# A gated mix of a 2-D Fourier filter and a Mish layer: the first four x tiles bypass the butterflies, the gate's exponential moves to GpSimd, and the order of all engines is written anew

## The chip, the cores and the metric

The kernel runs on one core of one Trainium2 chip. The metric is the device time of one execution in microseconds (us). Five engines work from queues of their own, each strictly in its written order: TensorE (PE in the profile; its weight loads are PEld), VectorE (DVE), ScalarE (ACT), GpSimd (POOL), and SyncE (SP), which only issues transfers.

## The reference

The input x has 2048 rows of 512. Two branches are mixed row by row by a gate:

```python
g = sigmoid((x * gate_w).sum(-1, keepdims=True))
X = rfft2(x);  a = irfft2(X * (w_r + 1j * w_i), s=(2048, 512))    # spectral branch
h = x @ w1 + b1                                                   # 512 -> 1792
act = h * tanh(log(1 + exp(h)))                                   # Mish
b = act @ w2                                                      # 1792 -> 512
out = g * a + (1 - g) * b
```

All tensors are bf16 in memory.

## The kernel before, in words

x is held as 16 tiles of 128 rows (tile t has rows t, t+16, t+32, ...). The work is cut into some 540 named tasks; each has a function that emits its instructions, the data it reads and writes, and an engine (some may go to one of two or three). What runs in which order is a text, `ORDER` (line 327): it lists the task names, and `place` (line 222) walks it once. Each task goes to the end of its engine's queue; `name:dve` picks the engine, `name::1` gives the slot of the buffer that the task opens. Three pairs of PSUM banks (pool `pr`), two single banks (`mm2`) and three SBUF buffers (`tmp`) are shared; a task that opens a slot waits for all users of its former holder. A GpSimd task waits for the GpSimd task before it, and for the last VectorE task marked `lock` that stands before it in the order. So an instruction that waits holds up everything behind it on its engine.

The tasks, in the order of the data:

- *Loads.* `x0` to `x3` bring four tiles each into rA, `w1_0` to `w1_2` the columns of w1, all on SP's queue; `cRF`, `braw`, `graw`, `cFD` (constants and biases) go over ScalarE's queue. `wr..s.` and `wi..s.` stage the filter weights in rE. `xt8` to `xt15` are transposing loads of x tiles 8 to 15, `w2_0`, `w2_1` load w2.
- *Warm-up.* `warm` is a row of 13 matmuls on zeros (line 537), fed by a memset `warm0` (line 526). `ones` and `ident` (lines 527, 529) build the identity matrix that transposes use.
- *Transposes.* `tr0` to `tr7` (line 603) turn tiles 0 to 7 on TensorE, `evx` copies them into xT.
- *Mish branch*, four chunks c of 512 rows: `mm1_c_f` (line 897, four matmuls of 512 columns for one of 14 blocks of 128 hidden features), `hc_f` (line 904 on VectorE, 908 and 909 on ScalarE: adds b1 to two blocks and empties a PSUM pair), `exp`, `ln`, `tanh` on ScalarE (lines 918, 920, 921), `mulc_half_tile` (line 933), `mm2_t_.._0` and `_1` (line 949: eight and six matmuls for one tile), `o` (line 966 or 963: times 1 - g).
- *Spectral branch, forward.* `bf` (line 618) forms on GpSimd the sum and the difference of the two halves of each row, x[0:256] +- x[256:512], the first step of the transform along the row. `p` (line 637) transforms each tile across its 128 rows, four matmuls of 128 columns for the sum and the difference, odd and even columns; `ep` empties PSUM; `d` (line 649) transforms along the row, `ed` empties it into rD. `s1w0` to `s1w3` write rD to a scratch in memory, four tiles each, and `s1r0` to `s1r3` read it back in another layout into rE, over the staged weights. So they wait for all copies that take the weights from there (`wrm...`, `wim...`, lines 684 and 685) as well. `wrn` duplicates the real part by a transfer within SBUF, `win` negates and copies the imaginary part on VectorE.
- *Filter.* `t` (line 762) is a 16-point transform, `et` empties it, `sa` and `sb` swap the halves of the partitions by DMA, `p1`, `p2`, `ad` (lines 776, 779, 782) multiply and add. An edge correction follows: `e1` (800, 801), `es0`, `es1` on ScalarE (809, 810), `xp1`, `xp2`, `ead` on VectorE (811, 812, 813), `e2` (820, 822), `e3` (826).
- *Backward.* `it` (line 837), `eit`, `id` (876), `ey`, and `ip` (line 975 for tiles 0 to 11; 957 for 12 to 15, accumulated into mm2's bank).
- *Gate.* `gate0` (tiles 0 to 11) and `gate12` (line 732), `zcl` clamps, `ez` is exp on ScalarE (line 743), `ez1` adds 1, `omg` is the reciprocal, `gcol` the product (749). `fa`, `fb`, `fin` (983, 987, 979) mix, `out` stores.

The h of chunk 2 goes into rD, which the scratch writes read: `h2_..` wait for all four `s1w`.

Of the kernel before, what the change touches and what calls it, by code (L numbers as in the profile page):

```python
# [10 lines left out]
AF = mybir.ActivationFunctionType  # L11
ALU = mybir.AluOpType
# [315 lines left out]
ones cRF x0 ident warm0 w1_0 wrp0 warm::0 braw wrp1 x1 graw w1_1 cFD w1_2 x2 x3 wr0s0 wr0s1 tr3::0 bf0_1:pool tr2::1 evx3:dve wr0s2 evx2:act tr1::0  # L328
wr1s0 tr0::1 bf2_0:pool evx1:act evx0:dve wr1s1 mm1_0_0::1 wi0s0 bf0_0:pool wi0s1 mm1_0_1 wi0s2 bf4_1:pool tr5::0 wi1s0 tr_b::1 p0::2 ev_b evx5:act p1
wi1s1 mm1_0_2::0 h0_0:dve xt8 mm1_0_3 ep0:dve bf4_0:pool mm1_0_4::1 h0_2:dve mm1_0_5 mm1_0_6::2 bf2_1:pool h0_4:dve exp0_0 p4::0 p5 mm1_0_7 bf8_1:pool  # L330
ep4:dve mm1_0_8::1 h0_6:dve p6::0 p7 mm1_0_9 bf12_0:pool ep6:dve exp0_4 mm1_0_10::2 h0_8:dve mm1_0_11 bf8_0:pool d6::0 d7 h0_10:dve d0::1 ed6:act
tr7::1 d1 tr6::0 evx7:dve mm1_0_12::2 exp0_8 evx6:dve bf12_1:pool ed0:dve mm1_0_13 p8::0 tr4::1 h0_12:dve p10::1 evx4:act p11 p9 xt9 wip1 ep8:act
ep10:dve wip0 p14::2 wrm101:pool p15 exp0_12 p2::0 p3 ep14:dve mm1_1_8::1 xt10 ln0_0 wrm110:pool mm1_1_9 ep2:dve d14::2 d15 h1_8:dve d2::0 xt11 d3
wim001:pool ed2:dve mm1_1_2::1 mm1_1_3 w2_0 ed14:dve wim111:pool d4::0 s1w0 ln0_8 d5 h1_2:dve d10::2 d11 w2_1 gate0::0 wrm111:pool ed10:dve mm1_1_4::1
tanh0_0 zcl0 mm1_1_5 ed4:dve wrm011:pool p12::2 p13 h1_4:dve mm1_1_6::0 s1w1 mm1_1_7 wrm010:dve mm1_1_0::1 wim000:dve ldM wrm000:dve mm1_1_1 rft
ep12:act wim101:dve mul0_0_3:dve h1_6:act d8::2 d9 mul0_0_0:dve mm2_3_0_0::1 mul0_0_1:dve ez0 tanh0_8 mul0_0_2:dve mm1_1_10::0 h1_0:dve wim100:pool
mm1_1_11 ed8:dve mm1_1_12::1 exp1_0 wim110:pool mm1_1_13 h1_10:dve s1w2 d12::2 d13 ez10 omg0 mm1_2_4::0 h1_12:act gcol0 mul0_1_0:dve mul0_1_1:dve
mm2_1_0_0::0 exp1_4 mul0_1_3:dve mul0_1_2:dve mm2_1_0_1 wrm100:dve exp1_8 ed12:dve wrn1 wim011:pool mm1_2_12::1 o1_0:dve s1w3 mm1_2_2::2 exp1_12
wrm001:dve mm1_2_3 win1:dve ln1_0 wrn0 mm2_2_0_0::0 wim010:dve win0:dve s1r0 mm1_2_5 s1r1 mm1_2_13 s1r2 wic1:dve wiz1:dve wic0:pool h2_2:dve s1r3
mm2_2_0_1 wiz0:pool wrc1:pool wrz1:pool edge h2_12:dve ln1_8 ldG mm1_2_6::2 wrc0:pool wrz0:pool mm1_2_7 o2_0:dve mm1_2_10::1 h2_4:dve tanh1_0 mm1_2_11  # L340
h2_6:dve mm1_2_8::0 h2_10:dve mm1_2_9 mm1_2_0::2 h2_8:dve mm1_2_1 t2_0::1 h2_0:dve xt12 t6_0::0 t6_1 tanh1_8 mul1_0_1:pool t2_1 mm2_0_0_0::0 et2:dve
xt13 t0_0::2 t0_1 mul1_0_0:dve t3_0::1 et6:act t3_1 mul1_1_1:dve mm2_0_0_1 sa2::0 mul1_0_3:dve sb2 et3:act sa6::1 t5_0::0 mul1_1_0:dve t5_1 sb6
o0_0:act t4_0::1 mul1_1_2:dve t4_1 et5:act sa3::2 mul1_1_3:dve mm2_3_0_1 sb3 et4:dve mul1_0_2:pool xt14 et0:act t7_0::0 t7_1 mm2_4_0_0::0 o3_0:dve
et7:act xt15 p2_2:dve exp2_0 mm2_4_0_1 p1_2:dve ad_2:dve t1_0::1 t1_1 p1_3:dve o4_0:act mm2_5_0_0::1 sa0::0 et1:act p2_3:dve sb0 p1_6:dve inv exp2_4
mm1_3_0::2 p2_6:dve mm1_3_2::0 ad_6:dve ad_3:dve mm1_3_12::1 sa1::1 exp2_8 p2_0:dve sb1 mm1_3_3 p1_0:dve sa4::2 mm2_5_0_1 sb4 ad_0:dve exp2_12
h3_2:dve sa5::0 gate12::0 ln2_0 sb5 mm1_3_13 p2_1:pool zcl12 o5_0:dve mm1_3_8::0 h3_12:dve mm2_6_0_0::0 p1_1:dve p2_4:dve mm2_6_0_1 p1_4:dve ln2_8
ad_4:dve mm1_3_4::1 p2_5:dve sa7::2 mm1_3_9 p1_5:dve sb7 ad_1:dve mm1_3_5 ez12 h3_8:dve ad_5:pool mm2_7_0_0::1 h3_4:dve tanh2_0 mm1_3_6::0 p1_7:dve
mm1_3_7 p2_7:dve mm2_7_0_1 ad_7:dve h3_6:dve e1::1 mm1_3_1 es0::1 mul2_0_0:pool es1 ez112 o7_0:act xp2 mm1_3_10::0 ezb12 xp1::0 tanh2_8 ead::2
mm1_3_11 o6_0:dve e2::1 mul2_0_3:pool h3_0:dve mm2_8_0_0::1 e3 exp3_0 h3_10:dve it5_0::2 it7_0::1 mul2_1_2:pool it7_1 it5_1 eit7:dve mm2_11_0_0::0
exp3_4 mul2_1_3:dve it3_0::0 eit5:dve it3_1 mul2_1_0:pool it6_0::1 it6_1 exp3_8 mm2_11_0_1 eit6:dve mul2_0_2:pool it2_0::2 it2_1 eit3:dve exp3_12  # L350
it1_0::1 it1_1 mm2_8_0_1 o11_0:dve ln3_0 mul2_0_1:pool it0_0::0 eit2:dve it0_1 mm2_10_0_0::0 eit0:dve it4_0::2 mul2_1_1:pool it4_1 o8_0:dve ezr1::0
# [10 lines left out]
LOADS = ["x0 w0 x1 w1 w2 x2 x3", "x0 x1 w0 w1 x2 w2 x3", "x0 w0 x1 w1 x2 w2 x3", "x0 w0 w1 x1 w2 x2 x3"]  # L362


def _build(nc, A_x, A_w_r, A_w_i, B_x, B_w1, B_b1, B_w2, gate_w, out, merge=12, xtp=8, xtl=12, loads=0, finb=11, nbf=0, u3=1, wdma=1):
# [10 lines left out]
    with es:  # L376
# [57 lines left out]
        warm = hs01[:, 1, 0:256]  # L434
# [5 lines left out]
        def bank(b, i=0):  # L440
            return ps[:, (2 * b.slot if b.pool == "pr" else 6 + b.slot) + i, :]
# [7 lines left out]
        def tb(b):  # L449
            return tmp[:, b.slot, :]  # L450
# [3 lines left out]
        def tf(b):  # L454
            return tmpf[:, b.slot, :]
# [70 lines left out]
        G.add("warm0", "pool", 0.2, lambda e: e.memset(warm, 0.0), "warm", writes=["warm"])  # L526
# [4 lines left out]
        NWARM = 13  # L531
        wb = _Buf("pr")

        def f_warm(e):
            ins = None
            for _ in range(NWARM):
                ins = e.matmul(bank(wb)[:, 0:256], warm[:, 0:128], warm, start=True, stop=True)
            return ins

        t_warm = G.add("warm", "pe", NWARM * 0.22, f_warm, "warm", reads=["warm"], writes=[wb])  # L540


        XG = [(0, 4), (4, 8), (8, 12), (12, 16)]
# [3 lines left out]
        def ld(name, *a, **kw):  # L547
            seq[0] += 1
            kw.setdefault("cls", "f_ld")
            return dma(name, *a, off=-0.01 * seq[0], **kw)  # L550

        def ld_x(i, **kw):
            a, b = XG[i]
            return ld(f"x{i}", x_sb[:, a:b, :], xv[:, a:b, :], 1.4 + 0.6 * (a == 0), writes=[("x", t) for t in range(a, b)], **kw)
# [5 lines left out]

        ld("cRF", cst[:, 0, :], d_front[:, 0, :], 0.2, writes=["cRF"], queue="act")
# [21 lines left out]
        for i, (a, b_) in enumerate([(0, 8), (8, 14)]):  # L583
            ld(f"w2_{i}", w2_sb[:, a:b_, :], w2v[:, a:b_, :], 0.39 * (b_ - a), cls="f_w2", nd=8 * (b_ - a), writes=[("w2", f) for f in range(a, b_)])
# [128 lines left out]
        dma("ldM", rF[:], d_M[:].rearrange("p f n -> p (f n)"), 5.6, "f_m", writes=["M"], deps=t_p[6:7])  # L713
        dma("rft", rft[:, :], d_inv[:, 0, :], 0.3, "f_late", writes=["rft"], deps=t_p[6:7])
        dma("ldG", rB[:], d_G[:].rearrange("p f n -> p (f n)"), 5.6, "f_late", writes=["G"], deps=t_p + t_s1w)
# [6 lines left out]
        for t0, t1 in ((0, 12), (12, 16)):  # L722
            gb = _Buf("mm2")
# [19 lines left out]
            add("ez", 0.3, lambda e, c_=c_: e.activation(ez[:, c_], zcl[:, c_], AF.Exp), ["zcl"], ["ez"], eng="act", tab="et")  # L743
# [3 lines left out]
            add("omg", 0.2, lambda e, c_=c_: e.reciprocal(omg[:, c_], gcol[:, c_]), ["gcol"], [("omg", t) for t in range(t0, t1)])  # L747
            if t0 < merge:
                add("gcol", 0.17, lambda e, c_=c_: e.tensor_tensor(out=gcol[:, c_], in0=ez[:, c_], in1=omg[:, c_], op=ALU.mult),
                    ["ez"] + [("omg", t) for t in range(t0, t1)], ["gcol"] + [("gc", t) for t in range(t0, t1)])  # L750
# [297 lines left out]
```

## Time and profile before

| what | us |
|---|---|
| median of 4 runs | 146.05 (144.88 to 146.13) |
| the profiled execution | 144.88 |
| its span (first to last instruction) | 142.9 |
| TensorE busy | 132.1 |
| VectorE busy | 119.6 |
| ScalarE busy | 112.8 |
| GpSimd busy | 63.3 |
| first transpose, first mm1 matmul | 5.41, 8.26 |
| last group of matmuls begins | 139.42 |

The profile is of one execution. A line of the timeline gives start, duration, engine, source line, operation, output and input, shape and count; in brackets stands the idle time of the engine before the line and what ended it. Durations of matmuls overlap, so the distance from one start to the next is their true cost. Two bf16 instructions of VectorE that follow each other overlap a little as well: the 1.22 us of an evacuation of 1024 columns cost 1.14 in a row.

### The profile page before, as it was taken

How to read it: one execution, taken by the hardware profiler on the slowest of the kernel's cores; microseconds unless marked ns; L12 is line 12 of the kernel's file. 1: busy time of each engine (PE TensorE's matmuls, PEld its weight loads, DVE VectorE, ACT ScalarE, POOL GpSimd, SP SyncE). 2: the span in 40 equal slices, each digit the busy share in tenths (PEclk: the TensorE clock that was granted, in tenths of full speed). 3: DMA queues.
4: the chain of work that ended last, by engine and by line, in shares of the span. 5: the costliest groups of instructions: out<-in, count | busy, mean ns of one | idle time of the engine just before them, and what ended most of it. 6: DMA issues, size and time to landing. Idle time of an engine off the chain costs nothing.

```text
span 142.9 us, 2342 instructions
## 1 busy us (share of the span) xinstructions
PE 132.1 (92%) x905; PEld 73.7 (52%) x921; DVE 119.6 (84%) x154; ACT 112.8 (79%) x77; POOL 63.3 (44%) x50
## 2 busy tenths in 40 slices
PE   4789999889969999998999999998699999999992
PEld 3435556657534544444665454443366567655561
DVE  0117999999999998897968999997999989899772
ACT  2211557899999999999899999998499999945470
POOL 4499996799607250304150040509639700003510
PEclk9999999999999999999999999999999999999999
DMA  3999999999979959999999680300000000000554
GB/s 103 324 373 391 169 162 165 92 216 324 281 182 408 253 116 224 318 339 399 339 231 105 162 206 8 73 0 0 0 0 0 5 0 0 0 5 0 220 197 173
DMA packets 22991, 23.45 MB, mean 164 GB/s; under 512 B 13828, under 2 KB 19716, under 8 KB 22404
## 3 DMA queue, kind: packets, MB, share of 16 engines
q1 hardware_dynamic: 22512, 23.07, 63.0%
q10 hardware_dynamic: 468, 0.23, 0.6%
q8 instruction: 7, 0.11, 0.3%
q14 instruction: 4, 0.03, 0.1%
HBM read 14.89 MB, written 4.19 MB: 134 GB/s over the span
## 4 chain that ended last, share of the span: by engine, by line
PE 68%; ACT 11%; DMA 8%; DVE 7%; issue 3%; SPq 2%; DVEq 0%
PE ps L949 30%; PE ps L897 19%; PE ps L876 5%; DMA rE<-scr 5%; ACT uT L920 4%; DMA rA<-in_A_x_dram 3%; PE ps L837 3%; PE ps L762 3%; ACT uT L921 3%; PE ps L603 2%; SPq L477 2%; DVE rA L697 2%; PE ps L975 2%; PE ps L637 2%; PE ps L649 1%
## 5 line engine op out<-in xcount | busy, mean ns | idle before, releaser
L897 PE MATMUL ps<-rX,w_sb 128*128 128x512 bf16 x216 | 51.7, 385 | 1.4 <-DVE rX L514 0.5
L949 PE MATMUL ps<-w_sb,hs 128*128 128x512 bf16 (+1 forms) x178 | 39.5, 362 | 0.2
L897 PEld LDWEIGHTS ps<-rX,w_sb 128*128 128x128 bf16 x224 | 21.5, 99 | 26.1 <-issue 1.5
L949 PEld LDWEIGHTS ps<-w_sb,hs 128*128 128x128 bf16 x182 | 17.5, 98 | 17.4 <-DVE hs L933 0.3
L904 DVE TENSOR_TENSOR hs<-ps,b1f 128x1024 bf16<-128x1024 f32 x19 | 23.2, 1226 | 1.1 <-PE ps L897 0.6
L920 ACT ACTIVATE uT<-uT 128x4096 bf16<-128x4096 bf16 (+1 forms) x6 | 19.1, 3190 | 0.1
L921 ACT ACTIVATE uT<-uT 128x4096 bf16<-128x4096 bf16 (+1 forms) x6 | 19.1, 3187 | 0.1
L618 POOL TENSOR_TENSOR rB<-rA 128x1024 bf16<-128x1024 bf16 (+1 forms) x10 | 17.3, 1734 | 4.0 <-DMA rA<-in_A_x_dram 3.3
L918 ACT ACTIVATE uT<-hs 128x2048 bf16<-128x2048 bf16 (+1 forms) x8 | 13.6, 1694 | 5.5 <-DVE hs L904 5.3
L933 POOL TENSOR_TENSOR rD<-rD,uT 128x1024 bf16<-128x1024 bf16 (+1 forms) x7 | 13.4, 1918 | 7.1 <-ACT uT L921 3.4
L949 PE MATMUL ps<-w_sb,rD 128*128 128x512 bf16 x53 | 12.7, 379 | 0.2
L983 ACT ACTIVATE tmp<-ps,gcol 128x512 bf16<-128x512 f32 x11 | 7.2, 686 | 6.6 <-PE ps L975 6.0
L987 POOL TENSOR_TENSOR rX<-rX,tmp 128x512 bf16<-128x512 bf16 x3 | 3.5, 1152 | 19.2 <-ACT tmp L983 15.3
L966 DVE TENSOR_SCALAR rX<-ps,omg 128x512 bf16<-128x512 f32 (+1 forms) x13 | 9.2, 705 | 1.4 <-PE ps L949 1.2
L514 DVE CAST rC<-ps 128x1024 bf16<-128x1024 f32 x8 | 9.6, 1217 | 0.8 <-PE ps L762 0.8
L514 DVE CAST rA<-ps 128x1024 bf16<-128x1024 f32 x8 | 9.5, 1217 | 0.6 <-PE ps L876 0.6
L514 DVE CAST rF<-ps 128x1024 bf16<-128x1024 f32 x8 | 9.5, 1212 | 0.2 <-PE ps L837 0.2
L904 DVE TENSOR_TENSOR rD<-ps,b1f 128x1024 bf16<-128x1024 f32 x7 | 8.3, 1218 | 1.5 <-PE ps L897 0.8
L918 ACT ACTIVATE rW<-hs 128x2048 bf16<-128x2048 bf16 (+1 forms) x4 | 6.8, 1698 | 2.2 <-DVE hs L904 2.0
L514 DVE CAST rD<-ps 128x1024 bf16<-128x1024 f32 x7 | 8.4, 1210 | 0.0
L517 ACT ACTIVATE rC<-ps 128x1024 bf16<-128x1024 f32 x8 | 8.0, 1017 | 0.4 <-PE ps L762 0.2
L933 POOL TENSOR_TENSOR hs<-hs,uT 128x1024 bf16<-128x1024 bf16 x2 | 4.3, 2127 | 8.9 <-ACT uT L921 5.4
(95 smaller groups left out, 191.2 us busy)
## 6 DMA issues: line engine op xcount, KB each, us to landing
rA<-in_A_x_dram SPq DMA_DIRECT2D x4, 512.0 KB, 9.1
scr<-rD SPq DMA_DIRECT2D x4, 512.0 KB, 5.7
rF<-c_m SPq DMA_DIRECT2D x1, 2048.0 KB, 11.5
rE<-scr SPq DMA_DIRECT2D x4, 512.0 KB, 6.3
rB<-c_g SPq DMA_DIRECT2D x1, 2048.0 KB, 11.4
tmp<-rC SPq DMA_DIRECT2D x16, 128.0 KB, 2.5
out_dram<-rX SPq DMA_DIRECT2D x7, 256.0 KB, 2.3
w_sb<-in_B_w_dram SPq DMA_DIRECT2D x2, 768.0 KB, 9.4
```

Of the source, the lines that this page charges most:

```text
L514: return e.tensor_copy(out=o(), in_=i())
L517: return e.activation(o(), i(), AF.Copy)
L618: return e.tensor_tensor(out=xu[:, a:b_, uv, :], in0=x_sb[:, a:b_, 0:256], in1=x_sb[:, a:b_, 256:512], op=ALU.add if uv == 0 else ALU.subt ...
L897: ins = e.matmul(bank(b, i), w1_sb[:, dt_, 128 * ft:128 * (ft + 1)], xT[:, c, dt_, :, :], start=(dt_ == 0), stop=(dt_ == 3))
L904: return e.tensor_tensor(out=hs[hb][:, ft:ft + 2, :], in0=pair(b).rearrange("p (f s) -> p f s", f=2), in1=b1f[:, ft:ft + 2].unsqueeze(2).t ...
L918: return e.activation(o, hsf[hb][:, 512 * a:512 * b_], fn_)
L920: return e.activation(o, o, fn_, bias=1.0)
L921: return e.activation(o, o, fn_)
L933: return e.tensor_tensor(out=v, in0=v, in1=uvs[c][:, a:b_, 128 * tl:128 * (tl + 1)], op=ALU.mult)
L949: ins = e.matmul(bank(b)[:, 0:hi - lo], hs[hb][:, ft, 128 * tl:128 * (tl + 1)], w2_sb[:, ft, lo:hi], start=(ft == 0), stop=(ft == NFT - 1))
L966: return e.tensor_scalar(out=bs[:, t, lo:hi], in0=bank(b)[:, 0:hi - lo], scalar1=omg[:, t:t + 1], scalar2=None, op0=ALU.mult)
L983: G.add(f"fa{t}", "act", act(512) + 0.09, lambda e, t=t, b=b, z=z: e.activation(tb(z)[:, 0:512], bank(b), AF.Copy, scale=gcol[:, t:t + 1]) ...
```

## The change

Five edits go together.

1. *No butterflies for tiles 0 to 3* (`nbf=4`). The tasks `bf0_0`, `bf0_1`, `bf2_0`, `bf2_1` are gone. `p0` to `p3` take x itself: each of the four results is accumulated from two matmuls, one per half of the row, the second with the negated matrix NRF for the difference. NRF is loaded into `rft` by a new transfer `cNRF`, and `rft`'s later content now waits for the scratch writes.
2. *Loads.* Tiles 0 to 3 come as two loads of two tiles: `x0` first on SP's queue, `x1` first on ScalarE's. The others are now `x2` to `x4`.
3. *Warm-up.* The zeros and their memset are gone; 14 matmuls of 256 columns run on the identity, as soon as that is built. The bias tasks no longer wait for the warm-up.
4. *Gate.* `ez` is no longer exp on ScalarE but a power, e to the z, on GpSimd (`tensor_tensor` with `pow`); the base is written by two new memsets, `ec0` and `ec12`. `gcol`, `xp2` and `ead` are marked `lock`.
5. *A new ORDER* for all engines, and with it other choices of engine.

```diff
-def _build(nc, A_x, ..., merge=12, xtp=8, xtl=12, loads=0, finb=11, nbf=0, u3=1, wdma=1):
+def _build(nc, A_x, ..., merge=12, xtp=8, xtl=12, loads=0, finb=11, nbf=4, u3=1, wdma=1):
...
-        G.add("warm0", "pool", 0.2, lambda e: e.memset(warm, 0.0), "warm", writes=["warm"])
...
-                ins = e.matmul(bank(wb)[:, 0:256], warm[:, 0:128], warm, start=True, stop=True)
+                ins = e.matmul(bank(wb)[:, 0:256], identt[:, :], identt[:, :].unsqueeze(1).to_broadcast([128, 2, 128]), start=True, stop=True)
...
-        XG = [(0, 4), (4, 8), (8, 12), (12, 16)]
+        XG = [(0, 2), (2, 4), (4, 8), (8, 12), (12, 16)]
...
+        ld_x(1, queue="act")
         ld("cRF", cst[:, 0, :], d_front[:, 0, :], 0.2, writes=["cRF"], queue="act")
         if nbf:
             ld("cNRF", rft[:, :], d_front[:, 1, :], 0.2, writes=["rft"], queue="act")
...
-        dma("rft", rft[:, :], d_inv[:, 0, :], 0.3, "f_late", writes=["rft"], deps=t_p[6:7])
+        dma("rft", rft[:, :], d_inv[:, 0, :], 0.3, "f_late", writes=["rft"], deps=t_s1w)
...
+            G.add(f"ec{t0}", "pool", 0.1, lambda e, t0=t0, t1=t1: e.memset(omg[:, t0:t1], math.e), "w", writes=[(("omg", "c"), t0)])
...
-            add("ez", 0.3, lambda e, c_=c_: e.activation(ez[:, c_], zcl[:, c_], AF.Exp), ["zcl"], ["ez"], eng="act", tab="et")
+            add("ez", 0.35, lambda e, c_=c_: e.tensor_tensor(out=ez[:, c_], in0=omg[:, c_], in1=zcl[:, c_], op=ALU.pow), ["zcl", (("omg", "c"), t0)], ["ez"], eng="pool")
...
-        G.add("xp2", "dve", 0.29, ..., reads=wcs[2:4], writes=[e2_])
-        G.add("ead", "dve", 0.29, ..., reads=[e1_, e2_], writes=[ey_])
+        G.add("xp2", "dve", 0.29, ..., reads=wcs[2:4], lock=True, writes=[e2_])
+        G.add("ead", "dve", 0.29, ..., reads=[e1_, e2_], lock=True, writes=[ey_])
```

The new order, engine by engine, where it matters below:

- TensorE begins `warm tr1 tr0 tr2 tr3 mm1_0_2 tr5 tr6 p2 p0 p1 mm1_0_3 tr7 p3 mm1_0_6 mm1_0_7 tr_b mm1_0_0 mm1_0_1 mm1_0_4 mm1_0_5 d2` (before: `warm tr3 tr2 tr1 tr0 mm1_0_0 mm1_0_1 tr5 tr_b p0 p1 mm1_0_2`). In the middle stand `p6 p7 gate0 d4 d5 p12 p13 d6 d7 mm1_1_0 d12 mm1_1_1 mm1_1_10 d13 mm1_1_11 d10 d11 mm1_2_0 mm1_2_1 p8 p9 d0 d1 mm2_1_0_0 d8 mm2_3_0_0`, later `mm2_2_0_1 mm1_2_3 mm2_0_0_0 mm1_2_6 mm1_2_7 mm1_2_4 mm1_2_5 mm1_2_12 mm1_2_13 t6_0`. Around the edge: `mm2_5_0_1 mm2_9_0_0 e1 mm2_10_0_0 mm2_9_0_1 e2 mm2_10_0_1 it2_0` (before: `mm2_7_0_1 e1 mm1_3_1 mm1_3_10 mm1_3_11 e2 mm2_8_0_0 it5_0`).
- VectorE: `h1_4 ep6 zcl0 ep12 ed6 ez10 omg0 h1_0 ed12 ed10 h1_10 mul0_0_1`; `h1_12 o3_0 ed8 o1_0 wim000 wim100 win1 win0 o2_0 h2_0 h2_2`; at the edge `h3_4 h3_6 xp1 h3_10 xp2 mul2_1_2 ead mul2_0_0 e3 o9_0 ezb12`.
- ScalarE: `exp0_12 ln0_0 ln0_8 ed4 tanh0_0 tanh0_8 ep8 ed0 exp1_0`; `tanh2_8 o5_0 exp3_0 es0 es1 exp3_4 exp3_8 exp3_12 eit2 ln3_0 eit7 ln3_8 tanh3_0`. `h1_6`, `h1_12` and `ep12` go from ScalarE to VectorE.
- GpSimd begins `wrp1 ones ident ec12 ec0 wrp0 bf4_0 bf4_1`; `ez0` stands between `wrm001` and `wrm010`, `ez12` between `mul2_1_1` and `mul2_1_0`.
- SP: `xt11 w2_1 w2_0 ldM s1w1 wrn0 s1w3 s1w0 wrn1 s1w2 s1r0 s1r1 s1r3 s1r2 ldG edge rft` (before: `xt11 w2_0 s1w0 w2_1 s1w1 ldM rft s1w2 wrn1 s1w3 wrn0 s1r0 s1r1 s1r2 s1r3 edge ldG`).

## The prediction

> **What bounds the kernel now.** I read the page's totals and slices first, then TensorE's timeline from end to end, then the other engines around each hole in it.
>
> ```profile
> PE 132.1 (92%) x905; PEld 73.7 (52%) x921; DVE 119.6 (84%) x154; ACT 112.8 (79%) x77; POOL 63.3 (44%) x50
> ...
> PEclk9999999999999999999999999999999999999999
> ```
>
> TensorE is the bound on average, with VectorE close behind. Since its work is nearly fixed, only its holes can be gained, and the timeline names them:
>
> ```profile
> 1.80 2.95 PE L537 MATMUL ps<-hs 128*128 128x256 bf16 x13 [1.80 <-POOL hs L526]
> 5.41 2.33 PE L603 MATMUL ps<-identt,rA 128*128 128x128 bf16 x16 [0.66 <-DMA rA<-in_A_x_dram]
> 8.26 3.01 PE L897 MATMUL ps<-rX,w_sb 128*128 128x512 bf16 x8 [0.52 <-DVE rX L514]
> ...
> 41.65 0.62 PE L649 MATMUL ps<-cst,rC 128*128 128x128 bf16 x8 [1.13 <-ACT rC L517]
> ...
> 66.52 1.05 PE L762 MATMUL ps<-rE,rF 128*128 128x128 bf16 x16 [0.41 <-DMA rE<-scr]
> ...
> 101.03 0.20 PE L820 MATMUL ps<-tmp,rD 128*128 128x1 bf16 x2 [1.61 <-DVE tmp L813]
> ```
>
> [...] From the first transpose at 5.41 to the last matmul at 140.25 are 134.8 us; 2.65 us of evacuation and output follow, and the execution took 144.88 against its span of 142.9, so 1.98 us lie outside it.
>
> Weight loads show a loss that the brackets don't:
>
> ```profile
> 8.66 0.15 PEld L897 LDWEIGHTS ps<-rX,w_sb 128*128 128x128 bf16 x1 [0.28 <-issue]
> 9.09 0.15 PEld L897 LDWEIGHTS ps<-rX,w_sb 128*128 128x128 bf16 x1 [0.28 <-issue]
> ```
>
> They come 0.427 us apart until 10.4; the 16 matmuls of the same size from 79.16 to 82.61 come 0.216 us apart. TensorE runs at half speed up to about 10.4 us, although the granted clock reads full. A 128-column matmul costs 0.056 us (t, 16 in 66.52 to 67.41), half speed 0.107.
>
> The hole at 101.03 is made by GpSimd:
>
> ```profile
> 96.50 6.11 POOL L933 TENSOR_TENSOR rD<-rD,uT 128x1024 bf16<-128x1024 bf16 x3 [3.37 <-ACT uT L921]
> 97.47 1.30 DVE L812 TENSOR_TENSOR tmp<-tmp,wsi 128x128 f32<-128x128 f32 x1 [0.87 <-ACT tmp L810]
> 99.08 1.90 DVE L813 TENSOR_TENSOR tmp<-tmp 128x128 bf16<-128x128 f32 x1
> 102.80 6.94 ACT L918 ACTIVATE rW<-hs 128x2048 bf16<-128x2048 bf16 x4 [2.00 <-DVE hs L904]
> ```
>
> xp2 (L812) and ead (L813) take 1.30 and 1.90 us while GpSimd multiplies; xp1, of the same shape but with one operand in PSUM, took 0.28. Each ends about where one of GpSimd's multiplications ends. So 1.0 + 1.6 us of VectorE are stall, e2 waits 1.6 us for them, and h3_0 behind them keeps ScalarE idle for 2.0 us.
>
> **Part 1, loads and warm-up.** Landing in the old kernel:
>
> ```profile
> rA<-in_A_x_dram SPq DMA_DIRECT2D x1, 512.0 KB, 4.6
> w_sb<-in_B_w_dram SPq DMA_DIRECT2D x1, 512.0 KB, 6.3
> ```
>
> x0 landed at 5.36 and w1_0, issued at 1.25, at 7.5. Now x0 and x1 carry half each on two queues. By 5.4 the engines had moved some 0.9 MB (slices of half a microsecond: 190 to 370 GB/s from 2.0 on), of which x0 took half. Two quarter-megabyte loads beside w1_0 end between 4.2 (they go first) and 5.1 (all share equally); I take 4.7. Four transposes and their copies took 8.21 - 5.41 = 2.8 us, bound by two PSUM banks and copies of 0.42 to 0.6; they end near 7.5, where w1_0 lands too. So the first mm1 starts at 7.5 rather than 8.26. The extra issues (x1 0.39, cNRF 0.36 on ScalarE's queue) push ScalarE's table load, 2.69 to 3.97 today, to about 4.7; its first copy is due at 6.5. A warm-up matmul costs 0.213 us. It now waits for the identity, which GpSimd builds after one 0.27 us memset: 1.37 + 0.27, so fourteen run from about 1.7 to 4.7. GpSimd's two new memsets come after and stand in front of an addition that waits for x2 until 9.1.
>
> [...] the 2.9 us of half-speed work that I see up to 10.4 would shrink by 1.4. By the row, 2.95 us of warm-up, 0.66 of idleness and gappy transposes did not release it until 10.4. The new transposes have the same gaps, so I take 0 and keep the 1.4 for the range.
>
> **Part 2, no butterflies for four tiles.** GpSimd loses four additions of 1.15 us, 4.6 in all; TensorE gains 16 matmuls: 16 x 0.056 = 0.9 us, up to 1.7 if all were cold. GpSimd isn't the bound; what it buys is that p0 to p3 need only x, so that they fill TensorE at 9 to 13 us.
>
> **Part 3, the new order, by checkpoints.** I walk down TensorE's new queue with 0.865 us for an mm1 task, 1.73 / 1.30 for mm2 halves, 0.45 for two p or d, and let it wait for a PSUM pair where VectorE's queue (1.14 to 1.22 us per evacuation) frees it later.
>
> At 35.35 the new queue has finished d4 and d5. Against the old at 34.94 it has done four mm1 more (3.46), six d (1.35) and two p (0.45) less: 1.66 of useful work in 0.41 longer, **1.25 us ahead**. ScalarE's chain: exp0_12 ends near 26.4 (was 28.03), ed4 waits for d5 until 35.4, tanh0_8 ends at 44.1 (was 45.5).
>
> h1_6, h1_12 and ep12 move from ScalarE (2 x 1.27 and 0.92 off) to VectorE (3 x 1.14 on), ed6 too, ed0 and ed4 the other way; the walk carries them. From 36 to 44 VectorE sets the pace: h1_0, ed12, ed10 and h1_10 free the pairs; TensorE waits 0.4 before mm1_2_0 and 0.7 before p8. That is the old hole of 1.13, not removed but equalled.
>
> ed8 ends near 53.6, so s1w2 goes out then (s1w3 did at 51.67) and lands after the old 5.9 us at 59.5; s1r2 follows and lands near 66, as the last s1r did (66.17). Two waits stand here. h2_0 waits for s1w2 until 59.5, and on VectorE behind it stand all of h2, mul1 and the filter products; mm1_2_6 needs its pair at 60.9 and gets it at 60.7. rft, now behind ldG on SP's queue, is wanted only past 112, and w2 and M come in earlier than needed (mm2_1_0_0 at 44.5, t6_0). t6_0 waits for s1r2; TensorE reaches it at 66.1. By then it has done 14 mm2 matmuls more and 8 mm1 matmuls less than the old at 66.5: +1.3, and 0.4 earlier, **1.7 ahead**.
>
> From t6_0 to e2 the work is 16 mm1 tasks (13.85), 84 mm2 matmuls (18.15), t 3.6, gate 0.45, e1 0.3: 36.35, so e2 comes at 102.4. VectorE from h2_0 to e3: 39.9 us of instructions from 59.5, against 41.8 over 45.4 in the old; it fits with the old idleness of 3.6. The locks on xp2 and ead hold back GpSimd's next instruction, ez12, until they are done (behind ez12 stand mul2_1_0 and mul2_0_3, needed at 107 and 110), and mul2_1_1 ends near 100.3, before xp2 can start (exp3_0 stands before es0, so es1 ends near 100.9). xp2 and ead at 0.3 each with mul2_1_2 between finish at 102.0. e2 waits for nothing: the 1.6 us is the gain, **3.3 ahead**.
>
> After e2 remain 90 mm2 matmuls (19.4), it 3.6, id 7.0, ip 3.5, ezr 0.2: 33.7, plus the old 0.7 of small gaps: 136.9 instead of 140.25. What is late next is ScalarE: exp3_0 starts at 98 instead of 102.8, tanh3_0 ends near 119.8 with the two evacuations eit2 and eit7 added; mm2_12_0_0 can start at 120.5 and 15.6 us of work follow it. Both chains meet within half a microsecond.
>
> **Part 4, the power.** Off ScalarE go 0.22 and 0.21 us. GpSimd's own memsets and the power itself are not in the trace. Nearest row:
>
> ```profile
> L618 POOL TENSOR_TENSOR rB<-rA 128x512 bf16<-128x512 bf16 x4 | 4.6, 1151 | 3.3 <-DMA rA<-in_A_x_dram 3.1
> ```
>
> With 2.12 for 1024 elements this gives 0.18 + 0.0019 per element: 0.2 for twelve. Lower end 0.2. [...] the first TENSOR_TENSOR took as long as its sisters. By the row ez0 (zcl0 ends at 35.8) is done near 36.2, two microseconds before VectorE wants ez10; I take 0.4. [...]
>
> **Sum.** 1.25 by the front, 0.45 in the s1r stage, 1.6 at the edge: 3.3, less 0.3 for handovers a walk doesn't see: 3.0. The profiled 144.88 would become 141.9; the median of 146.05 becomes 143.0.
>
> **Rivals.**
> *Clock released early* (0.1): a further 1.4 off, 141.6. For it: the longer, later warm-up; against it: gaps between transposes.
> *Later scratch write takes the front's gain* (0.22): the second rW copy stands directly ahead of s1w2 in SP's queue, and in the old trace one such copy took 0.54 us to issue and one 2.64. With 2.64, h2_0 and t6_0 slip by 1.2 to 2, VectorE has no slack to return it: 144.2 to 145.
> *The split does not speed x* (0.1): landing still near 5.3 and w1_0 late, front gain near 0.4: 143.9 to 145.4, to no change with a second slip.
> *The power is slow* (0.06, slower): at c us each, VectorE loses c - 2.4 at ez10 and c - 1.2 at ezb12; beyond c = 3.4 the whole gain is gone, [...] against it the first-call row.
>
> **Numbers.** My forecast of 143.0 has 0.52. Its own spread is 142 to 144; for eight in ten I reach down for the clock and up for the slip: 141.2 to 145.4. Measurement tells about 1% (1.5 us). Faster by more: forecast, clock and most of the two slips, 0.84; within: 0.10; slower: 0.06.
>
> **What would show it.** Right: first mm1 at 7.3 to 7.8; t (L762 now) at 66 with more mm2 before it; no idle time ahead of e2, xp2 and ead at 0.3; last matmul near 137. Wrong: weight loads 0.2 apart before 10 us (clock); idle time ahead of mm1_2_6 (slip); VectorE waiting for GpSimd at ez10 or ezb12 (power).

## The result, and the profile after

The changed kernel takes **142.16 us** (median of 11 runs, 141.31 to 143.54); the kernel before took 144.84 beside it (16 runs, 142.93 to 146.13). The ratio is 0.986 with a 95% interval of 0.981 to 0.991: faster, by about 1.4%. The ratios in this document leave out executions more than 1.5% above a kernel's fastest, and of the kernel before that drops many, so they show less gain than the medians do; both are given. The profiled execution took 143.38, with a span of 141.7 (before 144.88 and 142.9).

Totals on the page of the changed kernel:

```profile
PE 132.8 (94%) x923; PEld 75.6 (53%) x938; DVE 118.4 (84%) x153; ACT 112.2 (79%) x73; POOL 61.7 (44%) x50
```

TensorE has 18 recorded matmuls and 0.7 us more, GpSimd 1.6 us less. What was to be gained were holes. TensorE's timeline in the changed kernel, at the places shown of before and at two new ones:

```profile
1.72 3.17 PE L534 MATMUL ps<-identt 128*128 128x256 bf16 x14 [1.72 <-POOL identt L527]
4.89 1.03 PE L601 MATMUL ps<-identt,rA 128*128 128x128 bf16 x8
7.85 1.87 PE L896 MATMUL ps<-rX,w_sb 128*128 128x512 bf16 x4 [0.73 <-ACT rX L516]
...
45.96 1.67 PE L948 MATMUL ps<-w_sb,hs 128*128 128x512 bf16 x7 [1.44 <-DVE hs L932]
...
67.74 0.61 PE L761 MATMUL ps<-rE,rF 128*128 128x128 bf16 x8 [0.23 <-issue]
...
103.92 0.19 PE L819 MATMUL ps<-tmp,rD 128*128 128x1 bf16 x2
```

The last line has no bracket: the 1.61 us before e2 are gone. The first mm1 starts 0.4 earlier. The hole of 1.13 at 41.65, which ScalarE ended, is gone as well, but another of 1.44 stands before `mm2_1_0_0`, and VectorE's multiplication (L932) ends it. GpSimd with both powers, and then VectorE, in the changed kernel's timeline:

```profile
36.28 2.30 POOL L742 TENSOR_TENSOR ez<-omg,zcl 128x12 f32<-128x12 f32 x1 [1.77 <-DVE zcl L740]
...
43.23 1.90 POOL L682 COPY rA<-rE 32x2064 bf16<-32x2064 bf16 x1
...
104.07 1.03 POOL L742 TENSOR_TENSOR ez<-omg,zcl 128x4 f32<-128x4 f32 x1 [2.02 <-DVE rD L932]
```

```profile
43.77 1.91 DVE L932 TENSOR_TENSOR hs<-hs,uT 128x1024 bf16<-128x1024 bf16 x1
```

The power takes 2.30 us for twelve columns and 1.03 for four. Behind it GpSimd is late, so that its copy `wim101` runs from 43.23 to 45.13. `mul0_0_1` starts on VectorE at 43.77, inside that copy, and takes 1.91 us; the median of the five multiplications from 43 to 48 is 0.68. `mm2_1_0_0` waits for it.

At the edge of the filter VectorE's two short instructions are short again:

```profile
102.44 0.28 DVE L811 TENSOR_TENSOR tmp<-tmp,wsi 128x128 f32<-128x128 f32 x1
...
103.11 0.28 DVE L812 TENSOR_TENSOR tmp<-tmp 128x128 bf16<-128x128 f32 x1
```

1.30 and 1.90 before, 0.28 each now. Last, the weight loads at the front:

```profile
8.23 0.15 PEld L896 LDWEIGHTS ps<-rX,w_sb 128*128 128x128 bf16 x1 [0.28 <-issue]
8.66 0.15 PEld L896 LDWEIGHTS ps<-rX,w_sb 128*128 128x128 bf16 x1 [0.28 <-issue]
```

Still 0.43 us apart: in this execution TensorE ran at half speed until 10.79. The granted clock does not tell; in a table of the same profile by stretches it reads 1.00 (the third number from the end):

```profile
core 0: us, PE busy (x) PEld busy (x) DVE busy (x) ACT busy (x) POOL busy (x), PEclk, DMA share, GB/s
...
8.00:11.00 3.00, 3.00 (x20) 1.94 (x19) 0.39 (x1) 0.60 (x1) 2.44 (x2) 1.00 1.08 367
```

The next section shows another execution of the same program, in which the half speed had ended before 5.20.

### The profile page after: what moved, and what is told of

Read it like the earlier page. It is cut to its first block, busy times and chain, and to the rows that moved or that the text cites. A ratio compares the mean times of both kernels' runs of the same rounds, so it can differ in the third digit from the quotient of the medians.

```text
span 141.7 us, 2368 instructions
## 1 busy us (share of the span) xinstructions
PE 132.8 (94%) x923; PEld 75.6 (53%) x938; DVE 118.4 (84%) x153; ACT 112.2 (79%) x73; POOL 61.7 (44%) x50
## 4 chain that ended last, share of the span: by engine, by line
PE 74%; DVE 13%; ACT 9%; issue 2%; POOL 1%; ACTq 0%; POOLq 0%
PE ps L948 31%; PE ps L896 27%; ACT uT L919 5%; DVE rF L513 3%; PE ps L761 3%; PE ps L875 2%; DVE rA L513 2%; PE ps L534 2%; DVE hs L932 2%; ACT uT L917 2%; PE ps L601 2%; PE ps L974 2%; DVE hs L903 2%; PE ps L647 1%; PE ps L836 1%
## 5 line engine op out<-in xcount | busy, mean ns | idle before, releaser
L903 DVE TENSOR_TENSOR hs<-ps,b1f 128x1024 bf16<-128x1024 f32 x21 | 25.0, 1217 | 0.5 <-PE ps L896 0.4
L616 POOL TENSOR_TENSOR rB<-rA 128x1024 bf16<-128x1024 bf16 x6 | 12.7, 2123 | 7.5 <-DMA rA<-in_A_x_dram 7.1
L986 POOL TENSOR_TENSOR rX<-rX,tmp 128x512 bf16<-128x512 bf16 x4 | 4.6, 1150 | 21.5 <-ACT tmp L982 18.2
L965 DVE TENSOR_SCALAR rX<-ps,omg 128x512 bf16<-128x512 f32 (+1 forms) x15 | 10.7, 715 | 3.0 <-PE ps L948 2.8
L932 POOL TENSOR_TENSOR rD<-rD,uT 128x768 bf16<-128x768 bf16 (+1 forms) x5 | 9.2, 1836 | 5.2 <-DVE zcl L740 4.8
L683 POOL TENSOR_SCALAR rW<-rE 32x2064 bf16<-32x2064 bf16 x4 | 7.6, 1906 | 7.1 <-DVE rA L683 6.8
L513 DVE COPY rX<-ps 128x512 bf16<-128x512 bf16 x4 | 1.7, 424 | 9.3 <-PE ps L601 9.3
L932 DVE TENSOR_TENSOR hs<-hs,uT 128x1024 bf16<-128x1024 bf16 (+1 forms) x14 | 9.3, 714 | 0.2 <-ACT uT L920 0.2
L513 DVE CAST rA<-ps 128x1024 bf16<-128x1024 f32 x7 | 8.3, 1217 | 0.3 <-PE ps L875 0.3
L948 PEld LDWEIGHTS ps<-w_sb,rD 128*128 128x128 bf16 x56 | 5.3, 98 | 5.2
```

Source lines behind the costliest of these rows:

```text
L513: return e.tensor_copy(out=o(), in_=i())
L616: return e.tensor_tensor(out=xu[:, a:b_, uv, :], in0=x_sb[:, a:b_, 0:256], in1=x_sb[:, a:b_, 256:512], op=ALU.add if uv == 0 else ALU.subt ...
L683: return e.tensor_scalar(out=o_, in0=i_, scalar1=1.0, scalar2=0.0, op0=ALU.mult, op1=ALU.add)
L903: return e.tensor_tensor(out=hs[hb][:, ft:ft + 2, :], in0=pair(b).rearrange("p (f s) -> p f s", f=2), in1=b1f[:, ft:ft + 2].unsqueeze(2).t ...
L932: return e.tensor_tensor(out=v, in0=v, in1=uvs[c][:, a:b_, 128 * tl:128 * (tl + 1)], op=ALU.mult)
L948: ins = e.matmul(bank(b)[:, 0:hi - lo], hs[hb][:, ft, 128 * tl:128 * (tl + 1)], w2_sb[:, ft, lo:hi], start=(ft == 0), stop=(ft == NFT - 1))
```

## The experiments

Each kernel was timed in turn with the kernel before, on the same chip; the three groups ran on three chips. Medians of the kernel before were 144.97 (11 runs) in the first group, 145.10 (43) in the second, 144.58 (11) in the third. *again* is of the first group only, so differences between it and kernels of the other groups lie across chips.

**First group: repeat, and three single edits of the changed kernel.**

*again*: the changed kernel, unedited.

> The changed kernel itself, once more, as the yardstick for the others of this call. 0.986 of the kernel before, as measured first (0.981 to 0.991); in its profile mul0_0_1 again takes 1.9 us and ez0 2.3.

141.73 (7 runs, 141.49 to 142.36), ratio 0.981 (0.976 to 0.986). TensorE at the front, in its profile:

```profile
5.20 0.62 PE L601 MATMUL ps<-identt,rA 128*128 128x128 bf16 x8 [0.31 <-DMA rA<-in_A_x_dram]
6.20 0.64 PE L601 MATMUL ps<-identt,rA 128*128 128x128 bf16 x8 [0.38 <-DVE rX L513]
7.58 1.02 PE L896 MATMUL ps<-rX,w_sb 128*128 128x512 bf16 x4 [0.73 <-ACT rX L516]
```

Eight transposes in 0.62 instead of 1.03 and four mm1 matmuls in 1.02 instead of 1.87, with the same program: the half-speed time ended before the first transpose. At the last group of matmuls *again* is 1.0 us earlier (137.09 against 138.11). The power (2.30), `mul0_0_1` (1.98) and the hole behind it (1.50) are as before. So one profile of the changed kernel can't stand for it, and profiles are best compared where both started alike. Its first 11 runs fall into seven of 141.31 to 142.22 and four of 143.13 to 143.54, and the profiled one with 143.38 is like the upper ones. Two of those four, though, have a granted clock of 0.986, so something other than the start can have made them long; they have no profile.

*wim_early*: is the copy that collides with `mul0_0_1` the cause of the hole?

```diff
-... wrm001:pool d5 p12::1 ...  tanh0_8 wim101:pool mm1_2_1 ...
+... wrm001:pool wim101:pool d5 p12::1 ...  tanh0_8 mm1_2_1 ...
```

> The changed kernel with one GpSimd copy (wim101) moved ahead of the power ez0, into the 1.8 us in which GpSimd waits for zcl0. Theory (the power's 2.3 us push wim101 onto mul0_0_1, and VectorE then waits for GpSimd): mul0_0_1 falls from 1.91 to 0.69 us, the hole of 1.44 us on TensorE before mm2_1_0_0 shrinks to 0.3, ed8 and the last scratch write come 1.2 us earlier, and the whole is 0.7 to 1.2 us faster than the changed kernel. Rival (mul0_0_1 waits for something else, or the time comes back at the scratch read): mul0_0_1 still long, or the total within 0.4 us of the changed kernel.

142.20 (6 runs, 141.93 to 142.51), ratio 0.984 (0.980 to 0.989): not faster than *again*. The mechanism held (five multiplications in 2.96 us, in *again* 4.25), the sum did not. The hole before `mm2_1_0_0` shrank to 0.20, but the 1.77 us in which GpSimd waits for `zcl0` are of the profile that started at half speed. In *again*, which was at full speed from the first transpose like this run, GpSimd waits only 0.15. So the copy pushed the power by almost its whole length. GpSimd in *again*, then here:

```profile
34.85 2.30 POOL L742 TENSOR_TENSOR ez<-omg,zcl 128x12 f32<-128x12 f32 x1 [0.15 <-POOL rW L682]
...
41.79 1.90 POOL L682 COPY rA<-rE 32x2064 bf16<-32x2064 bf16 x1
```

```profile
36.59 2.30 POOL L742 TENSOR_TENSOR ez<-omg,zcl 128x12 f32<-128x12 f32 x1
```

VectorE stood at `ez10`:

```profile
38.93 0.17 DVE L745 TENSOR_SCALAR gcol<-ez 128x12 f32<-128x12 f32 x1 [1.94 <-POOL ez L742]
```

TensorE's timeline of the same kernel shows where that went:

```profile
40.50 0.62 PE L647 MATMUL ps<-cst,rC 128*128 128x128 bf16 x8 [1.16 <-DVE hs L903]
```

The hole moved 5 us up. Here the power's 2.30 us on GpSimd held either the data that VectorE wants (1.94 us at `ez10`) or the copy behind it (1.50 us of hole in *again*); moving one gave the other.

*bf_back*: butterflies for tiles 0 to 3 back on GpSimd, the rest as changed.

```diff
-..., finb=11, nbf=4, u3=1, wdma=1):
+..., finb=11, nbf=0, u3=1, wdma=1):
...
-... x2 cNRF w1_1 ... tr3::1 wr0s2 ...
+... x2 w1_1 ... tr3::1 bf2_0:pool bf2_1:pool bf0_0:pool bf0_1:pool wr0s2 ...
```

> The changed kernel with the butterflies of the first four tiles put back (four additions on GpSimd ahead of bf4_0, p0 to p3 with four matmuls each, no cNRF). Theory (GpSimd is idle from 2.3 to 8.5 us, the additions end near 9.7 us, before p2 at 10.4; the bypass only adds 16 matmuls to TensorE): 0.6 to 0.9 us faster than the changed kernel. Rival (the bypass is what lets TensorE start early, as the prediction's part 2 had it): p2 or p0 waits for GpSimd, TensorE has a hole of 1 us or more near 10 us, and the total is 0.5 to 1.5 us slower than the changed kernel.

142.96 (6 runs, 142.27 to 143.22), ratio 0.989 (0.984 to 0.994), 1.2 above *again*. TensorE's timeline:

```profile
10.19 0.62 PE L635 MATMUL ps<-cst,rB 128*128 128x128 bf16 x8 [0.94 <-POOL rB L616]
```

The early p tasks now wait for the additions, 0.94 us, as the rival had it. The 16 matmuls saved give most of that back: the next transpose (`tr7`) comes only 0.25 later than in *again* (11.51 against 11.26), though x landed about 0.3 earlier. GpSimd, with 4.6 us more to do, starts the power 0.8 later (35.67 against 34.85). The bypass does buy something while the power is there.

*fill*: four extra matmuls on the identity in the gaps between the first transposes, to keep TensorE active.

```diff
+        fill("fl0", 1)      # each: n matmuls of 256 columns on identt, in pr's slot 0
+        fill("fl1", 3)
...
-... tr0::1 evx1:dve ... tr3::1 wr0s2 ...
+... tr0::1 fl0::0 evx1:dve ... tr3::1 fl1 wr0s2 ...
```

> The changed kernel with four more matmuls on the identity, one after tr0 and three after tr3, so that TensorE has no hole from 1.7 us to the first mm1. Theory [...] the four matmuls of mm1_0_2 0.22 us apart instead of 0.43, 1.0 to 1.4 us faster than the changed kernel. Rival (the holes don't matter, half speed lasts to 10.4 us or so whatever runs): no change beyond 0.3 us, or up to 0.2 slower.

142.29 (6 runs, 141.66 to 142.49), ratio 0.984 (0.979 to 0.990). Neither theory, whose early full speed was the author's guess, nor rival: not a gain, and 0.56 above *again*. In its profile TensorE had no hole from 1.72 to 7.5, and yet the transposes ran at half speed (eight in 1.03, from 4.91); full speed was there at the first mm1 (7.86). *again* and *wim_early* had it at the first transposes (eight in 0.62) without the filling. So the filled gaps did not fix the time at which half speed ended.

**Second group: the two suspected gains put alone into the kernel before, and the power taken out.**

*old_longwarm*: the kernel before with a warm-up that reaches x's landing.

```diff
-        NWARM = 13
+        NWARM = 17
```

> The kernel before with 17 warm-up matmuls instead of 13 and nothing else: they end near 5.4 us, when x0 lands (5.36), so the hole of 0.66 us before the first transpose is closed. Theory (the changed kernel's steady times and part of its gain come from the clock being released before the first mm1 in most executions, by a warm-up that reaches the transposes): its executions gather near the fastest of the kernel before, 143.0 to 143.6, within 0.6 us of each other, ratio 0.985 to 0.993. Rival (the clock is a matter of chance and the gain is in the order): median near 144.9, spread 143 to 146 as before, ratio 0.998 to 1.003.

143.51 (22 runs, 142.95 to 144.54), against 145.10: **1.6 us less by the medians**, though the ratio is 1.000 (0.998 to 1.003), as the rival had it. The two don't contradict each other. The 43 runs of the kernel before form two groups: 14 of 142.8 to 143.7 (median 143.2), and 29 of 144.7 to 146.4 (median 145.7). Of the second only the five lowest enter the ratio. With 17 matmuls, 21 of 22 runs lie between 142.9 and 143.8, where the first group is. TensorE's front in its profile:

```profile
1.80 3.81 PE L537 MATMUL ps<-hs 128*128 128x256 bf16 x17 [1.80 <-POOL hs L526]
...
8.13 1.90 PE L897 MATMUL ps<-rX,w_sb 128*128 128x512 bf16 x8 [0.52 <-DVE rX L514]
```

Eight matmuls in 1.90 us where they took 3.01. The two profiled executions (144.88 and 143.39) differ by 1.45 at `mm1_0_2` (12.21 against 10.76) and by 1.49 at their last group of matmuls (139.42 against 137.93), so the front is their whole difference. The second group goes up to 146.4, and what makes 24 of its runs longer than 144.9 no profile shows. Four more warm-up matmuls don't make the kernel faster than it could be; they make its faster case the usual one. Whether their number does it or the closed gap of 0.66 was not separated.

*old_longwarm_lock*: the same, and the two instructions at the edge marked.

```diff
-        G.add("xp2", ..., reads=wcs[2:4], writes=[e2_])
-        G.add("ead", ..., reads=[e1_, e2_], writes=[ey_])
+        G.add("xp2", ..., reads=wcs[2:4], lock=True, writes=[e2_])
+        G.add("ead", ..., reads=[e1_, e2_], lock=True, writes=[ey_])
```

> The same with xp2 and ead marked lock, as in the change (GpSimd's mul2_0_3 then waits for ead; mul2_0_0 still runs beside xp2). Theory of the edge: xp2 stays at 1.3 us, ead falls from 1.90 to 0.28, TensorE's hole before e2 shrinks from 1.6 us to 0.1, and the whole is 1.2 to 1.6 us faster than the kernel with the long warm-up alone. Rival (the time is given back behind the edge, by GpSimd's later multiplications or by VectorE): e2 comes earlier but the total is within 0.5 us.

141.97 (6 runs, 141.62 to 142.21), ratio 0.989 (0.983 to 0.995): **1.54 less again**. VectorE, and then GpSimd, at the edge:

```profile
97.98 0.29 DVE L813 TENSOR_TENSOR tmp<-tmp 128x128 bf16<-128x128 f32 x1
```

```profile
98.35 3.92 POOL L933 TENSOR_TENSOR rD<-rD,uT 128x1024 bf16<-128x1024 bf16 x2 [0.83 <-DVE tmp L813]
```

As expected, ead takes 0.29 where it took 1.90, xp2 stays at 1.30, GpSimd waits 0.83 for ead, and the hole before e2 is gone. Three small edits of the old kernel are as fast as the whole change.

*new_shortwarm*: the changed kernel with half the warm-up.

```diff
-NWARM = 14
+NWARM = 7
```

> The changed kernel with 7 warm-up matmuls instead of 14: they end near 3.2 us and leave a hole of 1.7 us before x lands. Theory of the clock: half speed until 10 us or later in most executions, 0.8 to 1.5 us slower than the changed kernel, or a wide spread. Rival (the clock is a matter of chance): the same median as the changed kernel within 0.3 us.

144.19 (22 runs, 142.90 to 145.46), ratio 1.002 (0.998 to 1.006), 2.5 above *again* and more than expected. TensorE's timeline:

```profile
5.09 1.03 PE L601 MATMUL ps<-identt,rA 128*128 128x128 bf16 x8 [1.68 <-DMA rA<-in_A_x_dram]
...
8.05 1.87 PE L896 MATMUL ps<-rX,w_sb 128*128 128x512 bf16 x4 [0.73 <-ACT rX L516]
```

TensorE rests 1.68 us before x lands, and its matmuls keep the pitch of half speed (0.43 us for 512 columns, 0.107 for 128) until about 12.0. At `tr7` it is 2.2 us behind *again* (13.45 against 11.26) and at its last group of matmuls still 2.0 (139.07 against 137.09). The other half microsecond of the medians these two profiles don't show.

*new_exp*: the changed kernel with the gate's exponential on ScalarE, as before, and two small VectorE instructions (`ez10`, `omg0`) moved to a later place.

```diff
-            add("ez", 0.35, lambda ...: e.tensor_tensor(..., op=ALU.pow), [...], ["ez"], eng="pool")
+            add("ez", 0.3, lambda ...: e.activation(ez[:, c_], zcl[:, c_], AF.Exp), ["zcl"], ["ez"], eng="act", tab="et")
...
-... tanh0_0 mm1_1_0::0 ez0 ed6:dve ... mm1_1_1 ez10 s1w1 omg0 ... e3 ez12 o9_0:dve
+... tanh0_0 ez0 mm1_1_0::0 ed6:dve ... mm2_1_0_1 ez10 omg0 o3_0:dve ... o5_0:act ez12 exp3_0 ... e3 o9_0:dve
```

> The changed kernel with the gate's exponential back on ScalarE (ez0 right behind tanh0_0, ez12 behind o5_0), and ez10 and omg0 moved on VectorE to just before o3_0, so that nothing waits for it. Theory (the power's 2.3 us on GpSimd cost about 1.2 us at mul0_0_1, whether by pushing wim101 or, with wim101 moved, by holding ez10): mul0_0_1 at 0.7 us, the hole before mm2_1_0_0 at most 0.4, total 0.7 to 1.3 us faster than the changed kernel. Rival (the slack returns at the scratch read or on ScalarE): within 0.4 us.

140.10 (6 runs, 140.00 to 140.53), ratio 0.976 (0.970 to 0.982): 1.6 below *again* by the medians. ScalarE, GpSimd and VectorE in its timeline:

```profile
40.03 0.20 ACT L742 ACTIVATE ez<-zcl 128x12 f32<-128x12 f32 x1
```

```profile
39.20 1.90 POOL L682 COPY rA<-rE 32x2064 bf16<-32x2064 bf16 x1
```

```profile
42.08 2.96 DVE L932 TENSOR_TENSOR hs<-hs,uT 128x1024 bf16<-128x1024 bf16 x5
```

The exponential costs ScalarE 0.20 us. `wim101` starts at 39.20, 2.59 earlier than in *again*, of which the power makes 2.30. The multiplications find no copy beside them (five in 2.96, in *again* 4.25), and TensorE has no hole before `mm2_1_0_0`, which starts at 42.82 instead of 44.52. Of these 1.7 us the two moved instructions can have about 0.2: by so much `mul0_0_1` starts earlier (42.08 against 42.26).

**Third group: what is the bypass worth by itself?**

*new_exp_bf*: *new_exp* with the edit of *bf_back*.

> The changed kernel with the exponential back on ScalarE as in new_exp and, besides, the butterflies of the first four tiles back on GpSimd as in bf_back. Theory (the bypass is worth what TensorE's hole before p2 costs less the 0.9 us of its extra matmuls; what bf_back lost beyond that was GpSimd's lateness at the power and wim101, which is gone now): within 0.4 us of new_exp. Rival (the bypass itself is worth 1.2 us, by an early p2): 1.0 to 1.3 us slower than new_exp.

140.41 (6 runs, 140.19 to 141.13), ratio 0.980 (0.973 to 0.987), as the theory had it. Its profiled execution started at half speed (four mm1 matmuls in 1.87), so the trace does not show the hole of *bf_back*.

*new_exp_again*: *new_exp*, repeated on the same chip.

> new_exp once more, as the yardstick of this call: 0.966 to 0.972 of the kernel before by medians, about 140.1 us, 1.6 us faster than the changed kernel.

140.01 (6 runs, 139.88 to 140.40), ratio 0.976 (0.969 to 0.983). It is the fastest version, 1.7 below *again* and, with its repeat, measured on two chips. Without the bypass it is 0.4 slower, at the edge of what these runs tell apart.

*old_lock_bypass*: the bypass alone, in the old order (on top of *old_longwarm_lock*).

```diff
-..., finb=11, nbf=0, u3=1, wdma=1):
+..., finb=11, nbf=4, u3=1, wdma=1):
...
-... cRF x0 ... tr3::0 bf0_1:pool ... wip1 ... wip0 p14::2 wrm101:pool p15 ... p2::0 p3 ep14:dve ... rft ... s1w3 ...
+... cRF cNRF x0 ... tr3::0 ... p14::2 p15 ... p2::0 p3 wip1 wip0 wrm101:pool ep14:dve ... s1w3 rft ...
```

> The kernel before with 17 warm-up matmuls and the two locks (as old_longwarm_lock) and, besides, the bypass of the butterflies for four tiles in the old order: bf0 and bf2 gone, p0 to p3 with eight matmuls each, cNRF loaded, rft behind the last scratch write, the two memsets of the wi pads behind p3. Theory (alone, in an order that does not use it, the bypass adds 16 matmuls to the bound engine): 0.4 to 0.9 us slower than old_longwarm_lock. Rival (taking 4.6 us off GpSimd is worth something in itself, by earlier weight copies and a shorter wait of p4 and p8): 0.5 us or more faster.

147.44 (6 runs, 147.09 to 149.25), ratio 1.032 (1.022 to 1.041), 5.5 above *old_longwarm_lock* by the medians: a clear loss that neither theory nor rival had. GpSimd's timeline:

```profile
27.47 0.53 POOL L672 MEMSET rA<- 128x32 bf16 x2 [4.14 <-PE ps L634]
28.16 1.90 POOL L683 COPY rW<-rE 32x2064 bf16<-32x2064 bf16 x1 [0.17 <-POOL rA L672]
```

The filter weights' buffer lies over x's. Once p reads x itself, the memsets of that buffer must wait for `p2` and `p3`, which the old order runs near 27; GpSimd stands still for 4.14 us, and its weight copies start at 28.16 instead of 25.09 (*old_longwarm_lock*). TensorE pays for it later:

```profile
43.13 2.92 PE L948 MATMUL ps<-w_sb,hs 128*128 128x512 bf16 x8 [1.73 <-DVE hs L932]
...
70.55 1.05 PE L761 MATMUL ps<-rE,rF 128*128 128x128 bf16 x16 [1.79 <-DMA rE<-scr]
```

The scratch round trip comes late as well. And TensorE, busy for only 0.72 of the 3 us from 40 to 43, then ran at half speed again, this time with a granted clock that says so, on the page and by stretches:

```profile
PEclk9999999999995999999999999999999999999999
```

```profile
44.00:45.00 1.00, 1.00 (x4) 0.31 (x3) 1.00 (x3) 0.64 (x1) 0.00 (x0) 0.50 0.96 410
```

It reads 0.50 from 44 to 47, the weight loads come 0.43 us apart, and some 1.7 us are lost (3.4 us at half speed, an estimate from this table). Five of the six runs have a mean granted clock of 0.977 to 0.988, the two longest (149.2) the lowest; but the sixth, at full clock, took 147.50, so the clock is not the whole loss. That the idle time caused the half speed was not tried. One part of this loss is the experiment's own: it also put `wrm101` behind the memsets. What it does show is that the bypass and the order that runs p0 to p3 at 9 to 13 us belong together.

## Why the prediction was right, and where its steps failed

Direction, size and range held: 143.0 was forecast for the median and 142.16 measured, 141.9 for the profiled execution and 143.38 measured. But that was partly luck: two steps failed in opposite directions, and the median is near the forecast partly because they cancel. Between the two profiles, both at half speed until after 10 us (10.4 and 10.79), the change brought 1.5 us and not the 3.0 of the sum; the hole of 1.44 behind the power is of the size of what is missing. The medians make up for it, as far as the groups of executions tell, because more of them start at full speed early. And the 146.05 that the forecast started from was the median of four runs; of 16 it is 144.84.

**Where the gain comes from.** By the medians the change is worth 144.97 - 141.73 = 3.2 us (2.7 in the first measurement). *old_longwarm* gives 1.6 for the warm-up alone, *old_longwarm_lock* 1.5 for the edge alone. The first is a matter of how often half speed ends early; by the ratio it is nothing (1.000). What remains to the changed kernel is 0.2: loads, bypass and new order bring about 1.9 (*old_longwarm_lock* 141.97 to *new_exp* 140.10), and the power takes 1.6 of it back (*new_exp* to *again*; some 0.2 of this is the moved `ez10` and `omg0`). Of the 1.9 the bypass has about 0.4. The 0.2 and the 1.6 lie across chips.

**Part 1, loads: right.** DMA answers for the changed kernel's front:

```profile
rA<-in_A_x_dram SPq DMA_DIRECT2D x1, 256.0 KB, 4.0
...
rA<-in_A_x_dram ACTq DMA_DIRECT2D x1, 256.0 KB, 4.2
...
w_sb<-in_B_w_dram SPq DMA_DIRECT2D x1, 512.0 KB, 5.7
```

Both loads were issued at 0.8, so x landed at 4.8 and 5.0 (forecast 4.7); in *again* it was 5.1 and 5.3. The first mm1 started at 7.85 or 7.58 (7.5). So the rival "the split does not speed x" is out for the first profile; in *again* the landing is hardly earlier than 5.36, but the loss that the rival named did not come.

**Part 1, clock: the step failed.** It took 0 from one row of before and kept for the range the 1.4 that an earlier end of half speed would save, the author's estimate from 2.9 us of half-speed work. But the row was one execution, and 14 of 43 runs of the kernel before are some 2.5 us faster than the other 29. The runs show that one kernel differs from run to run: two groups before (medians 143.2 and 145.7), nearly one with a warm-up up to x's landing (21 of 22 runs of *old_longwarm* between 142.9 and 143.8). That warm-up was worth 1.6 us by the medians, where the rival "clock released early" had 1.4 and a chance of 0.1. It is nothing to count on in a single execution: of the changed kernel, with 14 warm-up matmuls, one profile had full speed before 5.20, and the first, with no gap above 0.73 us from 1.72 on, stayed at half speed to 10.79. What decides between the two was not shown. For the changed kernel the pitch shows the two cases (eight transposes in 0.62 or in 1.03, one program). For the kernel before it is argued: its profile, at half speed to 10.4, is of the slower group, and none of the faster group was profiled.

**Part 2, the bypass: its direction right.** p0 to p3 do fill TensorE early, and without the bypass TensorE stands 0.94 us there (*bf_back*). By medians it is worth 1.2 with the power behind it and 0.4 without.

**Part 3: mostly right.** d5 ended at 35.66 (35.35). The edge's 1.6 came in full, e2 with no wait, xp2 and ead 0.28 (0.3). But the checkpoints from `t6_0` on are late by 1.5 to 2: 67.74 (66.1), e2 103.92 (102.4), last matmul 138.9 (136.9). The slip was there before the scratch write, and most of it comes with the hole behind the power: `mm2_1_0_0` started at 45.96 (44.5), ed8 ended at 54.84 (53.6), and `h2_0` started at 60.79 (59.5). The rival of a later scratch write named that place, but its cause, a slow rW copy in SP's queue, was not it: s1w2 went out as soon as ed8 was done (54.87 after 54.84).

**Part 4, the power: the term that was mis-sized.** From the row of an addition 0.2 was worked out and 0.4 taken; 2.30 and 1.03 were measured. With twelve and four columns that makes (2.30 - 1.03) / 8 = 0.16 us a column, if the first call cost nothing extra, and at most 1.03 / 4 = 0.26; 0.0019 was the row's. The wait at `ez10` was judged rightly: the two microseconds of slack just held it, the power ended at 38.58, and VectorE came to `ez10` at 38.62 without a pause. The step that fails is the one after: what stands behind the power on GpSimd. `wim101` was pushed onto `mul0_0_1`, 1.2 us of stall, 1.44 of hole. *wim_early* shows this mechanism, *new_exp* its price, 1.6 us by the medians where the sum had nothing. Both durations of the power came a second time in *again*. The rival "the power is slow", an estimate for which no row of before spoke, had looked at VectorE's waits at `ez10` and `ezb12`, with a loss only beyond 2.4; at 2.30 the loss came by another way.

A smaller miss has the same root. GpSimd's multiplications, moved behind the power at 104, run beside the gate's small VectorE instruction:

```profile
107.56 1.49 DVE L745 TENSOR_SCALAR gcol<-ez 128x4 f32<-128x4 f32 x1
```

It takes 1.49 where the same kind took 0.16 before, and two holes of 0.18 and 0.51 in front of `it` tasks follow on TensorE. That the one causes the others was not tried by itself; in *new_exp* the instruction takes 0.39.

**What stays open.** In the changed kernel `mul2_0_0`, which is marked too, stands right behind ead in the order, so whether the marks on xp2 and ead or the order protects them there was read from the order, not tried. The division of the 1.9 among loads and order was not measured either.

## What to carry to other kernels

An instruction moved to an idle engine is priced with what stands behind it: here GpSimd was 44% busy, and a power of 2.3 us still cost 1.6 us of the whole, because a copy behind it slid beside a VectorE multiplication. The two short VectorE instructions at the edge, with both inputs in SBUF, took 1.30 and 1.90 us beside GpSimd's multiplications and 0.28 each without, in the changed kernel; on the critical path such instructions deserve a held-back GpSimd, and two marks were worth 1.5 us. And a warm-up that ran up to the first real work made the early full speed the usual case here, though not the only one; it is judged by the spread of many executions, never by one profile. Two profiles are compared only when they started at the same speed: the 1.77 us of idle GpSimd that *wim_early* was to fill were there in one of them only.

## What the runs showed of the hardware

- A GpSimd power of 12 columns on 128 partitions took 2.30 us and one of 4 columns 1.03, 0.16 to 0.26 a column; an addition of 512 columns took 1.15 in the kernel before.
- Two VectorE instructions with two SBUF inputs took longer here beside a GpSimd instruction, and not without it: `mul0_0_1` 1.91 beside `wim101` in the changed kernel, where the median of its kind is 0.68 (with the copy elsewhere, in *wim_early*, five took 2.96 together); ead 1.90 beside a multiplication before and 0.29 with GpSimd held back in *old_longwarm_lock*. A `tensor_scalar` of one f32 input, at 107.56, took 1.49 beside a GpSimd multiplication too, and 0.16 before. How one engine holds up the other was not shown.
- At the start the granted clock read full (1.00 from 8 to 11 us in the changed kernel) while matmuls ran at half speed up to 10.79; their pitch told, 0.43 or 0.216 us for 512 columns. In the middle of *old_lock_bypass* the granted clock did show the half speed: 0.50 from 44 to 47, at the same pitch of 0.43.
- One program, the changed kernel, left half speed before 5.20 us in one execution (*again*) and at 10.79 in another.
